# A fused attention and four-expert kernel: g_norm loaded as one row, batch 0's key-value products in two banks, and chunk 7 of the first expert with a two-level down product

## The chip, the cores and the metric

The kernel runs on one core of a Trainium2 chip. A core has a matmul engine (TensorE, PE in the profile; PEld is its weight load), three engines for elementwise work (VectorE or DVE, ScalarE or ACT, GpSimd or POOL), and SyncE (SP), which here only issues DMA transfers; GpSimd issues some too. Data lies in HBM, in the on-chip SBUF (128 partitions), and in the accumulators of TensorE, the PSUM, which has eight banks. The metric is the device time of one execution in microseconds (us); the time before is 1660.72 us, the median of three runs (1660.16 to 1660.84).

## The reference

First a linear attention for 8 batches of 8 heads, 576 rows and 64 columns, then a sum of four experts over the 4608 rows of 512 columns that it makes:

```python
kv = np.einsum('bhsd,bhse->bhde', k, v)
out = np.einsum('bhsd,bhde->bhse', q, kv)
rms = np.sqrt(np.mean(out * out, axis=-1, keepdims=True) + 1e-06)
attn = out / rms * g_norm
x = attn.transpose(0, 2, 1, 3).reshape(B * S, H * D)

p = domain_probs / (domain_probs.sum(-1, keepdims=True) + 1e-09)
for e in range(4):
    h = np.maximum(x @ w1[e], 0.0)
    out += p[:, e:e + 1] * (h @ w2[e])
```

Everything is float32; w1[e] is 512 x 1024, w2[e] 1024 x 512. The two expert products hold nearly all the multiplications.

## The kernel before

**Tiling.** The rows are cut into nine chunks of 512: chunks 0 to 7 are the first 512 rows of each batch, chunk 8 collects the 64 rows that each batch has left. For each expert and each chunk there is an *up* product (x by w1, then relu) and a *down* product (h by w2, times the probability, added to the output). The four experts follow each other, so there are 36 steps s = 9 e + chunk; the down product of a step is keyed 1.2 steps later than its number, beside the up product of the next one.

**Products.** Both products use Winograd's form of Strassen's scheme: seven products of half-size blocks in place of eight. Up products do so at two levels from step 1 on (`up`: seven outer products of seven inner ones, each with 128 columns). Down products do so at one level in `down` (seven products of 256 columns, for each of two row halves) and at two levels in `down_deep` (49 products of 128 columns in groups of two outer products). Steps 1 to 7 are *mixed*: `down(..., mixed=True)` does five outer products at one level and hands the other two, (4, 2), to `down_deep`. From step 8 to step 34 all goes through `down_deep`. The price of a level is sums and differences of blocks before and after: those of x and h are made on VectorE and GpSimd (helper `combine`, line 501), those of w1 and w2 once per expert. `w2y` is the kind of buffer that holds the inner sums of a w2 block, seven of them per expert; `inner[e](products, key)` plans them.

**Opening.** The attention of batch 0 (`opening`) is written apart, since nothing is there to hide it. For each of four head pairs it loads q, k and v (SP, line 507, 288 KB each), turns q (line 801), sums the key-value products of both heads into one PSUM bank (line 816), turns the last 64 rows of q (line 820), copies the four 64x64 quadrants that q's product needs out of that bank, two by ScalarE (line 833) and two by VectorE (line 831), multiplies q by them (line 855), scales the rows by their inverse root mean square (`scaled`: squares on ScalarE, line 732; row sums on VectorE, line 739; root, lines 699 to 711; scaling, line 751), and turns the result (line 870) into x, where ScalarE multiplies by g_norm on the way out of PSUM (line 876). The first expert's up product of chunk 0 (`up_plain`, plain products of 512 columns) starts when the first pair is there. Until the first loads are in, TensorE is kept running by small products of an identity (line 1793). The attentions of batches 1 to 7 (`attention`) are made one chunk ahead, among the products: key-value product (line 1031), q's product (lines 1058 and 1067), row sums (line 971), scaling (line 980), turning (lines 1099 and 1120).

**g_norm and the probabilities.** g_norm's 64 values are wanted one per partition, in both halves, in `gcol`: `load_gains` (line 1733) issues two GpSimd transfers of 64 partitions by one element. `norm_probs` loads the probabilities into `p_all` by ten GpSimd transfers (lines 522 to 531), and VectorE divides each by its row's sum (lines 535 to 538).

**Order.** All work is entered as operations of a `Plan` with a key (the step, with a fraction), a cost for each engine that can do it, and the buffers read and written. `Plan.layout` derives a due time for each, and places them by a model of the engines, the DMA and the shared SBUF port (`port=True` keeps VectorE and GpSimd operations that share it apart; a GpSimd operation of this kind also waits for the last such VectorE instruction). For each step it tries `TRIES` = 8 random variations of the due times and keeps the one that leaves TensorE least idle. Buffers are assigned as the order is made: kinds such as `big`, `xf`, `small`, `w2y` and the PSUM kinds `u1`, `u2`, `db`, `ab` (two banks each) have a fixed number of slots; `later` lists memory that becomes slots of another kind once its first users are done. The program's order on every engine, and which of two engines does a sum, thus follow from the whole plan.

Of the kernel before, what the change touches and what calls it, by code (L numbers as in the profile page):

```python
# [41 lines left out]
class Plan:  # L42
# [51 lines left out]
    def layout(self, slots, later, idle, idle_banks, idle_until):  # L94
# [265 lines left out]
def kernel(  # L360
# [76 lines left out]
    for kind, n in BANKS.items():  # L437
# [22 lines left out]
        (("small", "q"), "w2y", [small_home[:, 2 * i * NT:2 * (i + 1) * NT] for i in range(2)]),  # L460
# [53 lines left out]
    def norm_probs(key):  # L514
# [257 lines left out]
    def opening(key, span, rem):  # L772
# [11 lines left out]
        for hp in range(NPAIR):  # L784
# [9 lines left out]
            bank, kbank = Buf("ab", f"qT{n}"), Buf("ab", f"kv{n}")  # L794
# [17 lines left out]
            def key_values(eng, bank=kbank, kt=kt, vt=vt, qt=qt):  # L812
                for j in range(J):
                    for r in range(2):
                        half, cols = slice(r * D, (r + 1) * D), slice(j * D, (j + 1) * D)
                        nc.tensor.matmul(  # L816
                            bank.ap[half, 0:D], lhsT=kt.ap[half, cols], rhs=vt.ap[half, cols],
                            start=(j == 0), stop=(j == J - 1), skip_group_check=True,
                        )
                nc.tensor.transpose(bank.ap[0:D, P:2 * P], qt.ap[:, (J - 1) * D:J * D], ident[:])  # L820

            plan.add(at(hp), {"PE": 1.3}, key_values, reads=[qt, kt, vt], writes=[kbank])
            left_q = Buf(None, f"ql{n}")

            def spread(eng, bank=kbank, to=kv, shift=0):
                for r in range(2):
                    c = r ^ shift
                    src = bank.ap[r * D:(r + 1) * D, 0:D]
                    dst = to.ap[c * D:(c + 1) * D, r * D:(r + 1) * D]
                    if shift:  # L830
                        done = nc.vector.tensor_copy(out=dst, in_=src)
                    else:
                        done = nc.scalar.activation(out=dst, in_=src, func=ACT.Copy)
                return done

            plan.add(at(hp), {"ACT": 0.42}, spread, reads=[kbank], parts=[kv])
            plan.add(
                at(hp), {"DVE": 0.35}, lambda eng, spread=spread: spread(eng, shift=1),
                reads=[kbank], parts=[kv],
            )  # L840
# [3 lines left out]
                    out=qT.ap[0:D, NT:NT + P], in_=bank.ap[0:D, P:2 * P], func=ACT.Copy),  # L844
                reads=[kbank], parts=[left_q], holds=[qT],
            )
            lefts.append(left_q)
            raw = Buf("raw", f"raw{n}")

            def attend(eng, raw=raw, kv=kv, qT=qT):  # L850
                for i in range(2):
                    for r in range(2):
                        for c in range(2):
                            half, at = slice(c * D, (c + 1) * D), r * HN + i * P
                            nc.tensor.matmul(  # L855
                                raw.ap[c][:, (2 * i + r) * D:(2 * i + r + 1) * D],
                                lhsT=qT.ap[half, at:at + P], rhs=kv.ap[half, r * D:(r + 1) * D],
                            )

            plan.add(at(hp + 0.4), {"PE": 0.7}, attend, reads=[qT, kv], writes=[raw])  # L860
# [887 lines left out]
    for e in range(E):  # L1748
        for i in range(NCH):
# [95 lines left out]
```

## Time and profile before

| | before |
|---|---|
| median of three runs | 1660.72 us |
| the profiled execution | 1657.95 us |
| its span, first to last instruction | 1656.2 us |
| PE busy | 1647.5 us (99% of the span) |
| DVE / ACT / POOL busy | 1232.4 / 980.0 / 701.4 us |
| read from HBM / written | 153.95 / 74.19 MB |

The profile is of one execution. A group's name says line, engine, operation, and output<-inputs by the program's names. A wait's row says who waited for whom, the total in us, how often, and the longest. Matmuls overlap, so one that is listed with 1.04 us for 16 passes takes less from its start to the start of the next; a float32 matmul is listed as two passes. Line numbers are those of the kernel before unless "after" is said; in the changed kernel the same lines lie up to 17 further down.

### The profile page before, as it was taken

The page shows a single profiled execution, that of the slowest core. Times are in us where ns is not written, and L with a number is a line of the kernel's source. Part 1 is how long each engine was busy: PE and PEld are TensorE (multiplying, and loading weights), DVE is VectorE, ACT ScalarE, POOL GpSimd, SP SyncE. Part 2 cuts the span into 40 slices and gives each one's busy share as a digit, 9 for nine tenths or more (in the row PEclk, how much of TensorE's full clock was granted, in tenths as well). Part 3 has the DMA queues.
Part 4 walks back from the last instruction along what each step waited for, and adds up shares of the span by engine and source line. Part 5 has one row for each costly group of instructions (what it writes and reads, how often), then busy time and mean ns, then how long its engine had stood idle before and what let it go on. Part 6 is the DMA issues. An engine that isn't in the chain of part 4 may idle for free.

```text
span 1656.2 us, 66292 instructions
## 1 busy us (share of the span) xinstructions
PE 1647.5 (99%) x28854; PEld 1557.0 (94%) x28854; DVE 1232.4 (74%) x2166; ACT 980.0 (59%) x2429; POOL 701.4 (42%) x665
## 2 busy tenths in 40 slices
PE   9999999999999999999999999999999999999998
PEld 5688888888899999999999999999999999999996
DVE  5777778776877778777778777777778787777774
ACT  3465555555456666666566666666666566666662
POOL 4443233223344454553345554343355545444341
PEclk9999999999999999999999999999999999999999
DMA  9875665524475354444558445444577544444442
GB/s 230 218 204 158 191 182 153 157 101 173 146 198 140 99 127 118 131 118 118 155 147 192 116 113 126 109 109 110 141 191 174 122 119 117 117 108 112 117 104 52
DMA packets 202763, 232.43 MB, mean 140 GB/s; under 512 B 92840, under 2 KB 142440, under 8 KB 202472
## 3 DMA queue, kind: packets, MB, share of 16 engines
q1 hardware_dynamic: 178856, 191.41, 38.4%
q0 software_dynamic: 23616, 36.78, 14.3%
q8 instruction: 226, 3.70, 0.9%
q14 instruction: 65, 0.53, 0.1%
HBM read 153.95 MB, written 74.19 MB: 138 GB/s over the span
## 4 chain that ended last, share of the span: by engine, by line
PE 97%; DMA 2%; SPq 1%; DVE 0%; issue 0%; ACT 0%; DVEq 0%
PE u L478 47%; PE db L478 32%; PE ab L478 15%; PE ab L1031 1%; PE ab L1099 1%; PE ab L1058 1%; DMA big<-in_moe_w_dram 1%; SPq L507 1%; DMA big<-in_q_dram 1%; DMA kv<-in_v_dram 0%; PE db L855 0%; PE db L1067 0%; PE ab L1120 0%; DMA kv<-in_k_dram 0%; PE ab L816 0%; PE ab L870 0%
## 5 line engine op out<-in xcount | busy, mean ns | idle before, releaser
L501 DVE TENSOR_TENSOR big<-big,big 128x1024 f32<-128x1024 f32 (+1 forms) x550 | 499.5, 927 | 27.2 <-ACT big L1296 12.0
L478 PE MATMUL u<-xf,big 128*64 128x128 f32 x7072 | 513.6, 273 | 0.0
L478 PEld LDWEIGHTS u<-xf,big 128*64 128x64 f32 x7072 | 412.9, 137 | 5.1 <-issue 0.7
L478 PE MATMUL u<-xf,w1y 128*64 128x128 f32 x5304 | 392.7, 273 | 0.0
L478 PE MATMUL db<-big,big 128*64 128x128 f32 (+1 forms) x4304 | 360.2, 308 | 0.5 <-ACT snap L1650 0.5
L1340 DVE TENSOR_TENSOR big<-u,snap 128x256 f32<-128x256 f32 x454 | 190.9, 422 | 206.3 <-PE u L478 150.7
L478 PEld LDWEIGHTS u<-xf,w1y 128*64 128x64 f32 x5304 | 310.6, 137 | 2.9 <-issue 0.8
L478 PEld LDWEIGHTS db<-big,big 128*64 128x64 f32 x4304 | 263.1, 137 | 40.8 <-issue 1.7
L1332 ACT ACTIVATE snap<-u 128x256 f32<-128x256 f32 x490 | 188.0, 384 | 183.2 <-PE u L478 160.3
L501 POOL TENSOR_TENSOR big<-big,big 128x256 f32<-128x256 f32 (+1 forms) x143 | 200.9, 1407 | 166.2 <-DVE big L501 81.2
L1332 ACT ACTIVATE big<-u 128x256 f32<-128x256 f32 x454 | 173.3, 383 | 66.0 <-PE u L478 41.9
L501 POOL TENSOR_TENSOR big<-big 128x512 f32<-128x512 f32 (+1 forms) x90 | 110.5, 1228 | 143.6 <-DVE big L501 88.7
L1650 ACT ACTIVATE snap<-db 128x256 f32<-128x256 f32 (+1 forms) x230 | 82.5, 359 | 136.9 <-PE db L478 123.3
L1296 ACT ACTIVATE big<-big 128x1024 f32<-128x1024 f32 x134 | 140.9, 1051 | 5.6 <-DVE big L501 4.9
L1503 POOL DMA_DIRECT2D out_dram<-big x118 | 102.1, 1102 | 43.3 <-ACT big L1480 35.9
L1658 DVE TENSOR_TENSOR big<-ab,snap 128x256 f32<-128x256 f32 x166 | 69.9, 421 | 66.5 <-ACT snap L1650 35.7
L1332 ACT ACTIVATE u<-u 128x256 f32<-128x256 f32 x245 | 90.9, 372 | 35.8 <-PE u L478 24.3
L1688 POOL TENSOR_TENSOR big<-big 128x512 f32<-128x512 f32 x25 | 31.9, 1276 | 146.1 <-DVE big L501 128.5
L478 PE MATMUL ab<-big,big 128*64 128x128 f32 (+1 forms) x1344 | 93.8, 278 | 0.0
L501 DVE TENSOR_TENSOR big<-big 128x512 f32<-128x512 f32 (+1 forms) x114 | 90.3, 797 | 2.3 <-POOL big L501 1.8
L478 PE MATMUL db<-w2y,big 128*64 128x128 f32 x1248 | 91.8, 273 | 0.0
L1480 ACT ACTIVATE big<-big,p_all 128x256 f32<-128x256 f32 x192 | 90.9, 500 | 1.4 <-POOL big L1688 0.7
(200 smaller groups left out, 2360.4 us busy)
## 6 DMA issues: line engine op xcount, KB each, us to landing
xf<-x SPq DMA_DIRECT2D x104, 512.0 KB, 3.6
xf<-x_h SPq DMA_DIRECT2D x85, 256.0 KB, 3.3
xf<-x SPq DMA_DIRECT2D x78, 256.0 KB, 3.6
out_dram<-big POOLq DMA_DIRECT2D x78, 256.0 KB, 6.2
x<-xf SPq DMA_DIRECT2D x36, 512.0 KB, 3.4
big<-in_moe_w_dram SPq DMA_DIRECT2D x30, 512.0 KB, 6.1
x_h<-big SPq DMA_DIRECT2D x18, 512.0 KB, 3.5
big<-in_moe_w_dram POOLq DMA_DIRECT2D x18, 512.0 KB, 7.3
```

What stands on the lines that cost most here:

```text
L478: nc.tensor.matmul(out_[cols], lhsT=lhsT[:, cols], rhs=rhs, **kw)
L501: lambda eng: adder(eng).tensor_tensor(out=out_(), in0=a(), in1=b(), op=op),
L507: key, SPC, lambda eng: nc.sync.dma_start(out=dst(), in_=src), reads=reads,
L1031: nc.tensor.matmul(bank.ap[r * D:(r + 1) * D, o * D:(o + 1) * D], lhsT=ks[r], rhs=vs[r], start=(j == 0), stop=(j == len(sets) - 1), skip_g ...
L1296: lambda eng: nc.scalar.activation(out=b.ap[:], in_=b.ap[:], func=ACT.Relu),
L1332: lambda eng: nc.scalar.activation(out=where(), in_=ps.ap[:, 0:HN], func=ACT.Copy),
L1340: lambda eng: nc.vector.tensor_tensor(out=block(whole, a, t), in0=src.ap[:, 0:HN], in1=add_.ap[:], op=ALU.add),
L1480: lambda eng: nc.scalar.activation(out=cell(i, half), in_=ap(), func=ACT.Copy, scale=prob()),
L1503: nc.gpsimd.dma_start(out=dst, in_=cell(i)[parts, :], accum_op=ALU.add)
L1650: lambda eng: nc.scalar.activation(out=where(), in_=group_of(ps.ap), func=ACT.Copy),
L1658: lambda eng: nc.vector.tensor_tensor(out=cell(tq, dq), in0=group_of(src.ap), in1=group_of(add_.ap), op=ALU.add,),
L1688: lambda eng: adder(eng).tensor_tensor(out=whole(to), in0=whole(a), in1=whole(b), op=ALU.add),
```

## The change

Five edits to batch 0's start and one further on:

- g_norm is loaded by SP as one row of 64 values into the first partition of `p_all`'s memory, behind the first q, k and v. Two one-column matmuls against an identity turn it into a PSUM bank, VectorE copies it to `gcol`. The loads of the probabilities then wait for this turn.
- The two heads' key-value products go to two banks, of kinds `u2` and `u1` (before: one of kind `ab`). ScalarE copies both quadrants from the first bank, VectorE both from the second.
- q's product is two operations: one needs only the two quadrants on the diagonal of the copied block, the other the two beside it. For the first two pairs each product is cut into 64 columns of weights.
- The division of the probabilities is keyed 0.9 steps later and counts as a user of the shared port.
- For the steps below 3, forty variations are tried in place of eight.
- Step 7 (the eighth chunk of the first expert) goes through `down_deep` as a whole; its remaining five `w2y` sums are keyed at 6.8 in place of 8.2, and two `w2y` slots become free when `q` is done, and no longer only when `small` is done too.

```diff
-            for n in range(self.TRIES):
+            for n in range(self.TRIES * (5 if step < 3 else 1)):
...
-        (("small", "q"), "w2y", [small_home[:, 2 * i * NT:2 * (i + 1) * NT] for i in range(2)]),
+        (("q",), "w2y", [small_home[:, 2 * i * NT:2 * (i + 1) * NT] for i in range(2)]),
...
-            nc.vector.tensor_tensor(
+            return nc.vector.tensor_tensor(
...
-        plan.add(key, {"DVE": 1.5}, norm, reads=[probs], writes=[probs])
+        plan.add(key + 0.9, {"DVE": 1.5}, norm, reads=[probs], writes=[probs], port=True)
...
-            bank, kbank = Buf("ab", f"qT{n}"), Buf("ab", f"kv{n}")
+            bank = Buf("ab", f"qT{n}")
+            kbank = [Buf(f"u{2 - r}", f"kv{n}_{r}") for r in range(2)]
...
-                            bank.ap[half, 0:D], lhsT=kt.ap[half, cols], rhs=vt.ap[half, cols],
+                            bank[r].ap[half, 0:D], lhsT=kt.ap[half, cols], rhs=vt.ap[half, cols],
...
-            plan.add(at(hp), {"ACT": 0.42}, spread, reads=[kbank], parts=[kv])
-            plan.add(
-                at(hp), {"DVE": 0.35}, lambda eng, spread=spread: spread(eng, shift=1),
-                reads=[kbank], parts=[kv],
-            )
+            kv_own, kv_other = Buf(None, f"kvo{n}"), Buf(None, f"kvx{n}")
+            for other in range(2):
+                to, at_ = (kv_own, kv_other)[other], slice(other * D, (other + 1) * D)
+                for r in range(2):
+                    c = r ^ other
+                    plan.add(
+                        at(hp), {"DVE": 0.235} if r else {"ACT": 0.24},
+                        lambda eng, r=r, c=c, at_=at_, kbank=kbank, kv=kv: nc.vector.tensor_copy(
+                            out=kv.ap[c * D:(c + 1) * D, at_],
+                            in_=kbank[r].ap[r * D:(r + 1) * D, 0:D]) if r
+                        else nc.scalar.activation(
+                            out=kv.ap[c * D:(c + 1) * D, at_],
+                            in_=kbank[r].ap[r * D:(r + 1) * D, 0:D], func=ACT.Copy),
+                        reads=[kbank[r]], parts=[kv, to],
+                    )
...
-            def attend(eng, raw=raw, kv=kv, qT=qT):
+            raw, wide = Buf("raw", f"raw{n}"), D if hp < 2 else P
+
+            def attend(eng, raw=raw, kv=kv, qT=qT, other=0, wide=wide):
                 for i in range(2):
...
+                    for c in range(2):
+                        r, half = c ^ other, slice(c * D, (c + 1) * D)
+                        at = r * HN + i * P
+                        for g in range(0, P, wide):
                             nc.tensor.matmul(
...
+                                raw.ap[c][g:g + wide, (2 * i + r) * D:(2 * i + r + 1) * D],
+                                lhsT=qT.ap[half, at + g:at + g + wide],
+                                rhs=kv.ap[half, other * D:(other + 1) * D],
...
-    def load_gains(eng):
+    gain_row, gain_bank = probs, Buf("u1", "gain_bank")
+    grow = p_all[0:1].rearrange("p n e -> p (n e)")[:, 0:D]
+    plan.add(
+        -2.95, SPC, lambda eng: nc.sync.dma_start(out=grow, in_=g_norm.unsqueeze(0)),
+        writes=[gain_row], kb=1)
+
+    def turn_gains(eng):
         for i in range(P // D):
-            nc.gpsimd.dma_start(out=gcol[i * D:(i + 1) * D, :], in_=g_norm.unsqueeze(1))
-
-    plan.add(-2.85, {"POOL": 2.5}, load_gains, writes=[gains], kb=1)
+            nc.tensor.matmul(
+                gain_bank.ap[i * D:(i + 1) * D, 0:1], lhsT=grow, rhs=ident[0:1, 0:1])
...
-            if s == NCH - 1:
-                inner[e]((1, 6, 7, 5, 3))
+            if s == NCH - 2:
+                inner[e]((1, 6, 7, 5, 3), 6.8)
...
-            if NCH - 1 <= s < E * NCH - 1:
+            if NCH - 2 <= s < E * NCH - 1:
                 down_deep(s, e, c)
             else:
-                down(s, e, c, 1 <= s < NCH)
+                down(s, e, c, 1 <= s < NCH - 2)
```

More of the change, by code (lines that the diff above doesn't have):

```diff
@@ L816, in key_values @@
                         nc.tensor.matmul(
[L817 removed]
+                            bank[r].ap[half, 0:D], lhsT=kt.ap[half, cols], rhs=vt.ap[half, cols],
                             start=(j == 0), stop=(j == J - 1), skip_group_check=True,
                         )
[L820 to L822 removed]
+                nc.tensor.transpose(bank[1].ap[0:D, P:2 * P], qt.ap[:, (J - 1) * D:J * D], ident[:])
@@ L823, in opening @@
+            plan.add(at(hp), {"PE": 1.3}, key_values, reads=[qt, kt, vt], writes=kbank)
             left_q = Buf(None, f"ql{n}")
-            def spread(eng, bank=kbank, to=kv, shift=0):
+            kv_own, kv_other = Buf(None, f"kvo{n}"), Buf(None, f"kvx{n}")
+            for other in range(2):
+                to, at_ = (kv_own, kv_other)[other], slice(other * D, (other + 1) * D)
                 for r in range(2):
[L827 to L834, printed above, removed]
@@ L843, in opening @@
                 lambda eng, bank=kbank, qT=qT: nc.scalar.activation(
[L844 to L845 removed]
+                    out=qT.ap[0:D, NT:NT + P], in_=bank[1].ap[0:D, P:2 * P], func=ACT.Copy),
+                reads=kbank[1:], parts=[left_q], holds=[qT],
             )
             lefts.append(left_q)
[L848 to L850 removed]
+            raw, wide = Buf("raw", f"raw{n}"), D if hp < 2 else P
+            def attend(eng, raw=raw, kv=kv, qT=qT, other=0, wide=wide):
                 for i in range(2):
[L852 to L854 removed]
+                    for c in range(2):
+                        r, half = c ^ other, slice(c * D, (c + 1) * D)
+                        at = r * HN + i * P
+                        for g in range(0, P, wide):
                             nc.tensor.matmul(
[L856 to L860 removed]
+                                raw.ap[c][g:g + wide, (2 * i + r) * D:(2 * i + r + 1) * D],
+                                lhsT=qT.ap[half, at + g:at + g + wide],
+                                rhs=kv.ap[half, other * D:(other + 1) * D],
+                            )
+            plan.add(
+                at(hp + 0.4), {"PE": 0.36 if wide == D else 0.5}, attend, reads=[qT, kv_own], holds=[kv], writes=[raw])
+            plan.add(
+                at(hp + 0.4), {"PE": 0.36 if wide == D else 0.5}, lambda eng, attend=attend: attend(eng, other=1),
+                reads=[qT, kv_other], holds=[kv], parts=[raw])
             x = Buf("big", f"xg{n}")
@@ L1729 @@
     gains = Buf(None, "gains", gcol)
-    def load_gains(eng):
-        for i in range(P // D):
-            nc.gpsimd.dma_start(out=gcol[i * D:(i + 1) * D, :], in_=g_norm.unsqueeze(1))
-    plan.add(-2.85, {"POOL": 2.5}, load_gains, writes=[gains], kb=1)
+    gain_row, gain_bank = probs, Buf("u1", "gain_bank")
+    grow = p_all[0:1].rearrange("p n e -> p (n e)")[:, 0:D]
+    plan.add(
+        -2.95, SPC, lambda eng: nc.sync.dma_start(out=grow, in_=g_norm.unsqueeze(0)),
+        writes=[gain_row], kb=1)
+    def turn_gains(eng):
+        for i in range(P // D):
+            nc.tensor.matmul(
+                gain_bank.ap[i * D:(i + 1) * D, 0:1], lhsT=grow, rhs=ident[0:1, 0:1])
+    plan.add(-1.99, {"PE": 0.3}, turn_gains, reads=[gain_row], writes=[gain_bank])
+    plan.add(
+        -1.85, {"DVE": 0.15},
+        lambda eng: nc.vector.tensor_copy(out=gcol[:], in_=gain_bank.ap[:, 0:1]),
+        reads=[gain_bank], writes=[gains])
     opening(-2.0, 1.3, 0.1)
```

## The prediction

> **What bounds the kernel now.** I read the page first: busy time and the chain that ended last.
>
> ```profile
> span 1656.2 us, 66292 instructions
> PE 1647.5 (99%) x28854; PEld 1557.0 (94%) x28854; DVE 1232.4 (74%) x2166; ACT 980.0 (59%) x2429; POOL 701.4 (42%) x665
> ...
> PE 97%; DMA 2%; SPq 1%; DVE 0%; issue 0%; ACT 0%; DVEq 0%
> ```
>
> TensorE (PE) is busy or named as the cause nearly everywhere, so two things count: matmul work removed, and time at the ends in which TensorE does nothing useful. The waits of PE name the idle part (total, times, longest):
>
> ```profile
> PE ab L1793 <- POOL ident masks.py:199: 1.4, 1, 1.4
> PE ab L801 <- DMA big<-in_q_dram: 1.0, 1, 1.0
> PE ab L1099 <- DVE ss L971: 0.8, 1, 0.8
> PE db L478 <- ACT snap L1650: 0.5, 1, 0.5
> PE ab L1031 <- DMA kv<-in_v_dram: 0.3, 1, 0.3
> PE db L855 <- ACT kv L833: 0.2, 1, 0.2
> ```
>
> After 80 us only one wait of 0.5 us is left. Anything to win outside the products lies in the first 80 us. The chain in that stretch (start, length):
>
> ```profile
> 4.04 8.96 DMA big<-in_q_dram
> ...
> 14.80 1.20 PE ab L816 x36
> ...
> 16.66 0.36 PE db L855 x2
> 17.02 0.00 issue
> 17.02 1.14 PE db L855 x14
> ...
> 20.18 1.87 PE u L478 x8
> ```
>
> So the opening is paced by loads until about 14.8 us and by TensorE afterwards; the first eight expert passes end at 22.05. The stage view (length, then busy time; last DMA share and GB/s) shows that the loads do not run evenly:
>
> ```profile
> 4.50:7.50 3.00, 3.00 (x59) 2.59 (x56) 0.00 (x0) 0.60 (x1) 0.00 (x0) 1.00 0.61 160
> 7.50:16.50 9.00, 7.73 (x151) 6.55 (x147) 3.61 (x11) 4.22 (x14) 2.18 (x3) 1.00 1.05 395
> ```
>
> In the slow 3 us the software queue, which only the two g_norm loads use by then, is moving its packets: 61 of them between 3.8 and 7.5 us. The two loads were issued at 1.5 to 2.7 us and landed 5.4 and 6.0 us after issue.
>
> **The skill.** "TensorEngine Tiling (Array Packing)", "Tiling Modes" and "Key Properties": 64x64 gives four tiles, 64x128 two, and different tiles may load weights and multiply in parallel. The trace agrees: L1058 (64x64, four tiles) does 64 passes in 0.99 us, 15.5 ns each; L855 (64 rows by 128 columns) 16 in 1.04 us, 65 ns. "PSUM — Partial Sum Buffer", "PSUM bank collisions": two engines may not touch one bank and quadrant together. The timeline shows ScalarE starting its copies out of the bank only when VectorE's end, though it needs nothing of VectorE's:
>
> ```profile
> 8.77 0.47 DVE L831 COPY kv<-ab 64x64 f32<-64x64 f32 x2 [7.90 <-PE ab L820]
> ...
> 9.34 0.46 ACT L833 ACTIVATE kv<-ab 64x64 f32<-64x64 f32 x2 [2.24 <-DVE kv L831]
> ```
>
> "DMA: Bandwidth & Descriptors", "Rules for kernel authors": a strided last dimension costs a descriptor per element; g_norm laid along partitions is that, 128 of 4 bytes. "SBUF — State Buffer", "Who interferes with whom": a VectorE tensor_scalar can be blocked for a whole GpSimd instruction. Here L536, 36 elements wide, took 2.10 us beside a GpSimd add of 2.37.
>
> **Part by part.**
>
> *Chunk 7's down products.* Before: five of seven at 256 columns, two at two levels. The unit rows, from around 380 us, where the gap from one start to the next is the cost:
>
> ```profile
> 379.35 1.04 PE L478 MATMUL db<-w2y,big 128*64 128x128 f32 x16
> 380.23 0.61 PE L478 MATMUL u<-small,w1y 128*64 128x128 f32 x8
> ...
> 386.34 1.90 PE L478 MATMUL db<-big,big 128*64 128x256 f32 x16
> 388.07 0.61 PE L478 MATMUL u<-small,big 128*64 128x128 f32 x8
> ```
>
> 16 passes of 256 columns take 388.07 - 386.34 = 1.73 us, 108.1 ns each; 8 of 128 take about 0.437 us, 54.6 ns each. TensorE's instruction order, built for both kernels, has 80 fewer 256-column and 140 more 128-column instructions, two passes each: -160 x 0.1081 + 280 x 0.0546 = -17.30 + 15.29 = **-2.0 us**. Other product counts are equal, as is the number of returns from attention work to products (53), so nothing offsets it. The price is elsewhere: VectorE +24 instructions, ScalarE +10, by count. Step 7 has no attention left to do, and between 325 and 450 us VectorE was busy 16.4 to 21.0 us of each 25, so I cost it at nothing; without that cover, see the slower rival. The w2 sums for five products are only moved, a step earlier (their buffers are freed when q is done, no longer when q and small are).
>
> *Opening, loads.* g_norm becomes one 256-byte row on SP, behind the first v. SP's later issues move 0.47 us back (the issue step, 2.14 - 1.67); the third v load now waits for the first v's landing (6.8 us) instead of the first k's, 1.1 us later than before. Both hide behind queued loads: that v was 8.8 us from issue to landing. What leaves is the small packets. If they are what halves the rate, 3.0 us at 160 GB/s moves 480 KB, which 395 GB/s moves in 1.2 us: all loads behind land up to 1.8 us sooner. If they are not: 0. A loss is excluded down to the 0.47 us issue slot.
>
> *Opening, TensorE.* The key-value product keeps its two 64x64 tiles, so I leave it at 1.20 us (upper gain, if one shared bank was the limit: down to 36 x 0.0155 = 0.56 us, 0.6 us per pair). The copies now run on two engines from two banks: done about 0.5 us sooner. q's product for pairs 0 and 1 becomes 32 passes on four tiles, 32 x 0.0155 = 0.5 us for 1.04; pairs 2 and 3 stay at 1.04 in two operations. The g_norm turn, two one-column matmuls, falls in TensorE's wait for the second q (8.7 us); its VectorE copy of 64x1 per half stands ahead of the first row sum, at most 0.2 us, and the result is needed only at 18.8. GpSimd loses two issues (1.26 us) in a stretch where it waits for w1 until 12.3 anyway; p_all's ten loads now wait for the turn, long past, and go out one 2.36 us sum earlier.
> With loads unchanged: second q's product 13.7 to 14.25; third key-value from 14.65 (its v lands at 14.5) to 16.1; fourth q turned 16.6; first x turned 17.2; half a product 17.7; fourth key-value 19.15; other half 19.65; eight passes, 21.5. That is -0.55 against 22.05. With loads 1.8 us sooner TensorE becomes the limit from the first key-value on (its fillers end at 7.2 whatever lands): the same sums end at 19.85, -2.2. I take loads 1.2 us sooner: third key-value at 13.45, end at 20.4: **-1.65**. The row sums that x needs keep up: first x ready near 14.4.
>
> *The wait at 58.8.* TensorE waits 0.76 us there because VectorE first did a w2 sum held up to 51.1 us by late loads, then the probability norm with its 2.1 us blocked instruction. In the changed order that w2 sum is GpSimd's, and the norm counts as a user of the shared port. With the durations of before, its row sums of chunk 1 end near 47.4, the root (ScalarE, behind two relus) 48.8, the four small steps 49.6, the norm 50.9 (0.3 + 0.2 + 0.4 + 0.3) and the scaling 52.1, where it was 58.06; TensorE arrives near 56.4: **-0.76**, even with TensorE early (0 if VectorE is late again). GpSimd's four w2 sums end at about 58.3 as its third did before it began; they are used from 62 us on.
>
> Sum: -2.0 - 1.65 - 0.76 = -4.4. Against the profiled execution (1657.95 us; span 1656.2 and 1.75 around it) that is 1653.5; the runs' median lies 2.8 above that execution, so 1660.72 - 4.4 = **1656.3**. The tail, 5 us after the last matmul, has the same order of instructions in both.
>
> **Rivals.** (B) *Only the products shrink.* The packets are not what slows the loads, and what TensorE gains early it loses waiting near 60 to 80 us, where DMA share is 0.82 to 0.97 and a key load already costs 0.32. For it: DMA is that full. Against: most waits of SP there are on TensorE itself (6.8 us on L1099) and move with it. Time: 1660.72 - 2.0 - up to 0.55, about 1658.4.
> (C) *Slower: VectorE late in step 9.* More tries were allowed for the first steps, so the order after them is new everywhere. Adding durations of VectorE's rows (1.23, 0.69, 0.42, 0.28 us by width) between its up-product sums: the second half of step 9 holds 21.7 us of work, before 12.6, in about 21.4 us of products. At the usual 76% busy that takes 28.6 us, 7.2 too long: 1656.3 + 7.2 = 1663.5. It decides from 4.4 us on. Against: neighbouring halves hold 18.5 and 16.0, room to work ahead, and 21.5 us halves occurred before with no wait.
> (D) *More:* key-value products gain from two banks too, or the waits at 78 and 1626 us go: 1653.5 to 1655.
> That the change does not do what it says is excluded for the products by the counts.
>
> **Numbers.** A 0.48 (1655.0 to 1657.6, at 1656.3), B 0.24, C 0.19, D 0.09. The bound of 0.2%, about what a measurement of this kernel can tell from no change, is 3.3 us: 1657.4 and 1664.0. Faster: A's 0.45 and D, 0.54. Same: A's 0.03, B, 0.07 of C, 0.34. Slower: 0.12. Range 1654.8 to 1662.0: A, B, half of D, a quarter of C.
>
> **What would show it.** Right: the stage from 4.5 to 7.5 us near 395 GB/s; eight expert passes done near 20.4 us; no wait of L1105 on VectorE near 57; no 256-column db products for chunk 7 and TensorE still busy throughout 375 to 450 us. Wrong: a wait of PE on VectorE or GpSimd after 80 us, or a DMA wait of over 1 us before it.

## The result, and the profile after

| | before | after |
|---|---|---|
| median | 1659.84 us (15 runs, 1658.35 to 1660.89) | 1655.60 us (15 runs, 1653.56 to 1660.74) |
| the profiled execution, its span | 1657.95, 1656.2 us | 1657.52, 1655.8 us |

The ratio of after to before is 0.9979, with a 95% interval of 0.9972 to 0.9986: 3.5 us less by the ratio (2.3 to 4.6), 4.2 by the medians. The two profiled executions differ by only 0.4 us, since the one of before lies 1.9 us below its median and the one of after 1.9 above. So the two traces show which waits went and came, but the size of the opening's gain has to come from many executions.

Page of after, span and busy time, then the chain's shares:

```profile
span 1655.8 us, 66574 instructions
PE 1644.6 (99%) x29010; PEld 1559.3 (94%) x29010; DVE 1240.3 (75%) x2190; ACT 983.1 (59%) x2439; POOL 712.5 (43%) x665
...
PE 96%; DMA 2%; SPq 1%; issue 0%; DVE 0%; ACT 0%
```

TensorE is still the bound: 2.9 us less busy. The waits of PE in after (total, times, longest):

```profile
PE ab L1037 <- DMA big<-in_v_dram: 1.7, 1, 1.7
PE ab L1810 <- POOL ident masks.py:199: 1.4, 1, 1.4
PE ab L802 <- DMA big<-in_q_dram: 1.3, 1, 1.3
PE ab L1037 <- DMA kv<-in_v_dram: 1.0, 2, 0.8
PE u L478 <- ACT big L732: 0.6, 1, 0.6
PE db L478 <- ACT snap L1656: 0.5, 1, 0.5
PE u L817 <- DMA big<-in_v_dram: 0.3, 1, 0.3
```

The wait on VectorE (0.8 us, L1099 of before, L1105 now) is gone. In its place L1037, the key-value product of batches 1 and 2, waits for v. The stages of the opening (length, PE, PEld, DVE, ACT, POOL busy, clock, DMA share, GB/s):

```profile
4.50:7.50 3.00, 3.00 (x74) 2.71 (x72) 0.00 (x0) 0.60 (x1) 0.00 (x0) 1.00 1.04 346
7.50:16.50 9.00, 7.41 (x185) 6.26 (x181) 4.72 (x15) 5.21 (x17) 2.18 (x3) 1.00 1.02 378
```

The slow 3 us have gone from 160 to 346 GB/s. By queue, from 4.5 to 7.5 us (packets, MB, share of the 16 DMA engines), before and then after:

```profile
q1 hardware_dynamic: 232, 0.48, 59.5%
q0 software_dynamic: 54, 0.00, 1.1%
...
q1 hardware_dynamic: 516, 1.04, 103.7%
```

The prediction counts 128 descriptors of four bytes for the two g_norm loads. The trace shows packets, and the pages have 64 fewer on the software queue without these loads (23616 before, 23552 after and in experiment 3). In the slow stage they took 1.1% of the engines' time, and the large loads 59.5% in place of 103.7%. So the small packets did not crowd the large ones out by their own time: the engines stood partly idle. What holds the large loads up is not shown.

TensorE's timeline, six rows of the opening and of batch 1 (start, duration, in brackets the idle time before it):

```profile
8.95 0.69 PE L856 MATMUL db<-kv,big 64*64 64x64 f32 x32
9.47 1.23 PE L817 MATMUL u<-big,big 64*64 64x64 f32 x36
12.19 0.66 PE L802 MATMUL ab<-ident,big 128*128 128x128 f32 x4 [1.26 <-DMA big<-in_q_dram]
13.80 1.26 PE L817 MATMUL u<-big,big 64*64 64x64 f32 x36 [0.33 <-DMA big<-in_v_dram]
...
19.40 1.94 PE L478 MATMUL u<-big,big 128*64 128x512 f32 x8 [0.63 <-ACT big L732]
...
44.67 0.80 PE L1037 MATMUL ab<-big,big 120*64 120x64 f32 x20 [1.66 <-DMA big<-in_v_dram]
```

q's product of pair 0 takes 9.47 - 8.95 = 0.52 us for its 32 passes. The first eight expert passes end at 21.34 (before 22.05). The chain that ended last shows how the 1.66 us come about (start, length):

```profile
20.55 1.77 SPq L507
24.45 4.19 DMA big<-in_v_dram
29.28 1.45 SPq L507
31.85 5.51 DMA small<-in_q_dram
37.42 7.12 DMA big<-in_v_dram
```

SP's queue, with the sixteen small loads of q for the next batch in it, comes to the second v of batch 1 only at 37.42, just after a small load of q that was issued at 31.85 has landed, and that v lands 7.1 us later.

**Where the time went, by equal work.** The next table compares the start of the n-th pass of an up product with its start in the trace of before, in us; negative is earlier than before. Rows are chosen where both kernels have done equal product work, but for the last two, where those with the new chunk 7 have done 2.0 us less.

| up-product pass, and its time in before | after | after, again | row alone | all but chunk 7 | chunk 7 alone |
|---|---|---|---|---|---|
| first, 20.1 us | -0.70 | -2.17 | -0.97 | -0.93 | +4.13 |
| 101st, 50.4 us | +1.13 | +2.31 | -0.26 | -0.98 | +4.13 |
| 151st, 67.6 us | +0.18 | +1.36 | -0.13 | -1.92 | +3.14 |
| 793rd, 152.0 us | +1.07 | +2.16 | -0.07 | -1.07 | +3.47 |
| 3537th, 497.3 us | -0.91 | +0.17 | -0.07 | -1.08 | +1.48 |
| last, 1649.6 us | -0.34 | +0.74 | -0.07 | -1.08 | +1.98 |

All that differs between the two executions of the changed kernel comes before 80 us. From 152 to 497 us each kernel with the new chunk 7 gains 1.98 to 1.99 us (but for the one of experiment 8, whose own order loses 0.8 us in between), and no other gains anything. Afterwards those kernels give 0.25 to 0.6 us back, in steps of 0.1 to 0.25 us.

### The profile page after: what moved, and what is told of

The parts are those of the page before. It is cut to its first block, busy times and chain, and to the rows that moved or that the text cites. A ratio compares the mean times of both kernels' runs of the same rounds, so it can differ in the third digit from the quotient of the medians.

```text
span 1655.8 us, 66574 instructions
## 1 busy us (share of the span) xinstructions
PE 1644.6 (99%) x29010; PEld 1559.3 (94%) x29010; DVE 1240.3 (75%) x2190; ACT 983.1 (59%) x2439; POOL 712.5 (43%) x665
## 3 DMA queue, kind: packets, MB, share of 16 engines
q0 software_dynamic: 23552, 36.78, 14.7%
## 4 chain that ended last, share of the span: by engine, by line
PE 96%; DMA 2%; SPq 1%; issue 0%; DVE 0%; ACT 0%
PE u L478 47%; PE db L478 32%; PE ab L478 15%; SPq L507 1%; DMA big<-in_v_dram 1%; PE ab L1064 1%; PE ab L1105 1%; PE ab L1037 1%; DMA big<-in_q_dram 0%; DMA small<-in_q_dram 0%; DMA kv<-in_v_dram 0%; PE db L1073 0%; PE ab L1126 0%; DVE big L1493 0%; PE ab L910 0%
## 5 line engine op out<-in xcount | busy, mean ns | idle before, releaser
L478 PE MATMUL db<-big,big 128*64 128x128 f32 (+1 forms) x4152 | 342.5, 304 | 0.5 <-ACT snap L1656 0.5
L501 POOL TENSOR_TENSOR big<-big,big 128x256 f32<-128x256 f32 (+1 forms) x164 | 231.2, 1413 | 178.9 <-DVE big L501 76.3
L478 PEld LDWEIGHTS db<-big,big 128*64 128x64 f32 x4152 | 252.9, 137 | 36.6 <-issue 1.2
L501 POOL TENSOR_TENSOR big<-big 128x512 f32<-128x512 f32 (+1 forms) x99 | 124.1, 1254 | 190.6 <-DVE big L501 117.6
L1656 ACT ACTIVATE snap<-db 128x256 f32<-128x256 f32 x236 | 84.4, 358 | 137.4 <-PE db L478 124.9
L1509 POOL DMA_DIRECT2D out_dram<-big x112 | 97.5, 1121 | 43.1 <-ACT big L1486 35.1
L478 PE MATMUL db<-small,big 128*64 128x128 f32 (+1 forms) x1344 | 102.1, 274 | 0.0
L478 PE MATMUL ab<-big,big 128*64 128x128 f32 (+1 forms) x1392 | 97.8, 276 | 0.0
L478 PE MATMUL ab<-kv,big 128*64 128x128 f32 x1280 | 88.4, 273 | 0.0
```

What stands on the lines that cost most here:

```text
L478: nc.tensor.matmul(out_[cols], lhsT=lhsT[:, cols], rhs=rhs, **kw)
L501: lambda eng: adder(eng).tensor_tensor(out=out_(), in0=a(), in1=b(), op=op),
L1509: nc.gpsimd.dma_start(out=dst, in_=cell(i)[parts, :], accum_op=ALU.add)
L1656: lambda eng: nc.scalar.activation(out=where(), in_=group_of(ps.ap), func=ACT.Copy),
```

## The experiments

Each ratio is to the kernel before on the same chip, with its 95% interval; 0.001 is 1.66 us.

**1. All but chunk 7** (changed kernel, with the old chunk 7):

```diff
-            if s == NCH - 2:
-                inner[e]((1, 6, 7, 5, 3), 6.8)
+            if s == NCH - 1:
+                inner[e]((1, 6, 7, 5, 3))
...
-            if NCH - 2 <= s < E * NCH - 1:
+            if NCH - 1 <= s < E * NCH - 1:
...
-                down(s, e, c, 1 <= s < NCH - 2)
+                down(s, e, c, 1 <= s < NCH)
...
-        (("q",), "w2y", [small_home[:, 2 * i * NT:2 * (i + 1) * NT] for i in range(2)]),
+        (("small", "q"), "w2y", [small_home[:, 2 * i * NT:2 * (i + 1) * NT] for i in range(2)]),
```

> The changed kernel with chunk 7 mixed again as before (and the five w2 sums and the two w2y slots where they were); TensorE's order is the changed kernel's up to the sixth step. Theory (products are what counts): 2.0 us slower than the changed kernel, so a ratio to the kernel before near 0.999. Rival (the new orders at the start are what counts, the products hide behind something else): no slower than the changed kernel, ratio 0.998. From step 7 on the lag to the kernel before, at equal up products, stays what it was at step 6.

Measured: 1656.91 us, 0.9987 (0.9981 to 0.9994), 1.3 us above the changed kernel's ratio. From step 7 on its lag to the kernel before stays what it was (-1.07 and -1.08 in the table), as expected.

**2. Chunk 7 alone** (kernel before, with the same four edits the other way round):

> The kernel before with chunk 7 at two levels and nothing else of the change; TensorE's order is that of before up to the fifth step. Theory: 2.0 us faster than before (160 passes of 256 columns less, 280 of 128 more), ratio 0.9988, no new wait of TensorE in the steps 7 to 9. Rival (VectorE late in step 9): less than 1 us gained or a loss, with a wait of TensorE on VectorE or GpSimd between 400 and 520 us.

Measured: 1658.42 us, 0.9991 (0.9983 to 0.9999): 1.5 us faster (0.2 to 2.8). Its profiled execution began with 2.8 us of waits for q, and then the granted clock was 0.50 from 15 to nearly 22 us, whence the +4.13 above, but from 152 to 497 us it gains exactly 1.99. No wait of PE on VectorE or GpSimd appears after 80 us: the slower rival of the prediction, VectorE late in step 9, does not occur. The steps that give 0.5 us back come in this kernel (from +1.48 to +1.98 in the table) and in every other with the new chunk 7; all of these show 0.25 us or so of it between 642 and 648 us, and none of the kernels with the old chunk 7 does. So chunk 7 nets about -1.5, as timed. What the steps are stays open: the profile names no wait of PE between 600 and 1500 us.

**3. No g_norm loads** (kernel before; what it leaves out, its expectation says):

```diff
         for i in range(P // D):
-            nc.gpsimd.dma_start(out=gcol[i * D:(i + 1) * D, :], in_=g_norm.unsqueeze(1))
+        nc.gpsimd.memset(gcol[:], 1.0)
```

> The kernel before with the two g_norm loads left out: GpSimd sets the column to one instead, so the multiplication by g_norm is left out of the result. Instruction order and buffers are those of before. Theory (the small packets slow the loads): the stage from 4.5 to 7.5 us moves at least 330 GB/s where it moved 160, the third pair's q product begins about 1 us sooner, and the time is 0.5 to 1.5 us shorter. Rival (the slow stage is something else, such as the start of the loads): stage and time as before.

Measured: 1658.06 us, 0.9989 (0.9981 to 0.9997), 1.75 us by the medians, and 1.8 (0.5 to 3.2) by the ratio. The stage, in this kernel:

```profile
4.50:7.50 3.00, 3.00 (x73) 2.72 (x71) 0.00 (x0) 0.60 (x1) 0.00 (x0) 1.00 0.96 346
```

**4. The two strided loads back** (changed kernel, into a column that nobody reads):

```diff
+    gspare = const.tile([P, 1], F32, name="gspare")
...
         make_identity(nc, ident[:])
+        for i in range(P // D):
+            nc.gpsimd.dma_start(out=gspare[i * D:(i + 1) * D, :], in_=g_norm.unsqueeze(1))
```

> The changed kernel with the two strided g_norm loads issued by GpSimd as well, into a column that nothing reads. Theory (small packets): the stage from 4.5 to 7.5 us falls back to 160 to 200 GB/s, first expert passes about 1 us later than in the changed kernel, total 0.5 to 1.2 us more than it. Rival: stage and total as in the changed kernel. If the wait for the second pair's v of batch 1 (1.66 us at 42.9 in the changed kernel's profile) is what limits the start, the total stays equal though the stage slows down.

Measured: 1656.91 us, 0.9981 (0.9974 to 0.9988): by the ratio only 0.3 us above the changed kernel, by the medians 1.3. The same stage:

```profile
4.50:7.50 3.00, 2.61 (x57) 2.27 (x55) 0.00 (x0) 0.60 (x1) 0.00 (x0) 1.00 0.57 168
```

Experiments 3 and 4 switch the slow stage off and on by these two loads and nothing else: 346 GB/s without, 168 with them. In time, the loads' cost in the changed kernel is not shown: 0.3 us by the ratio is less than the 0.5 to 1.2 expected, but the intervals allow more. This profile has the wait for v of batch 1 too (1.6 us), and the expectation says that the total could then stay equal. The first expert pass starts 0.60 us earlier than before even with the slow loads. This compares one execution with one other, and two of the changed kernel differ by 1.47 us there, so it doesn't fix the worth of the opening's other edits.

**5. The row alone** (kernel before, with the g_norm row, its turn and its copy in place of `load_gains`, as in the diff of the change; nothing else):

> The kernel before with one part of the change: g_norm as one row, with its turn and copy; key-value products, q's product, norm, tries and chunk 7 as before. TensorE's and VectorE's order up to 60 us is that of before but for the turn, and the probabilities' loads stay behind two sums. The kernel before without any g_norm load was 1.75 us faster. Theory 'the packets are the opening's gain': the stage from 4.5 to 7.5 us moves 310 GB/s or more in place of 160, and the time is 1.2 to 1.9 us below before. Rival 'the turn and the row give it back': the stage is as fast, the time within 0.6 us of before.

Measured: 1658.17 us, 0.9988 (0.9981 to 0.9994): 2.0 us faster (1.0 to 3.2), which agrees with no loads at all. No loss by the turn and the row is seen. This gain rests on the timed runs: in the traces the row's first expert pass is 0.97 us early, and from the 793rd pass on only 0.07 us of that are left; a wait of 0.36 us for batch 1's second v is one part of the loss. In the row the number of pieces and the issuing queue (SP's for GpSimd's) change together. Which of the two matters was not tested. Its stage:

```profile
4.50:7.50 3.00, 3.00 (x68) 2.72 (x66) 0.00 (x0) 0.60 (x1) 0.00 (x0) 1.00 1.05 313
```

**6. One bank and one q product again** (changed kernel, with `key_values`, the copies and `attend` of before):

```diff
-            bank = Buf("ab", f"qT{n}")
-            kbank = [Buf(f"u{2 - r}", f"kv{n}_{r}") for r in range(2)]
+            bank, kbank = Buf("ab", f"qT{n}"), Buf("ab", f"kv{n}")
...
-            raw, wide = Buf("raw", f"raw{n}"), D if hp < 2 else P
+            raw = Buf("raw", f"raw{n}")
```

> The changed kernel with one part undone: the two heads' key-value products of batch 0 go to one bank of kind ab again, two copies by ScalarE and two by VectorE as before, and q's product is one operation of 128 columns of weights; the g_norm row, the order rules and chunk 7 stay. Theory 'TensorE's part of the opening counts' (the prediction's 0.55 us at equal loads): for pairs 0 and 1 two times 0.52 us come back, and the copies end 0.5 us later; eight expert passes end 0.5 to 1.1 us later than in the changed kernel's profile (21.27 us there), and the time is 0.5 to 1.1 us above the changed kernel's. Rival 'loads set the opening': TensorE waits for the second q at 12.2 us and for v at 13.5 us whatever comes before, so eight passes end within 0.3 us of 21.3 and the time is within 0.3 us.

Measured: 1656.52 us, 0.9982 (0.9975 to 0.9988), not to be told from the changed kernel. The first expert pass starts 1.03 us earlier than before, inside the spread of the kernels with the new products (0.04 to 2.17). The eight passes end at 21.02 us, as the "loads set the opening" rival expects, but not by the waits that it names: with the old products and fast loads (here and in experiments 3 and 5) TensorE waits for no load between 7 us and the first expert pass, which starts at 19.0 to 19.1. With the new products it waits for q and v and starts at 17.9 to 20.1, 19.0 in the middle. So the shorter products mostly wait for the next load, and no gain of theirs in time is shown.

**7. The division of the probabilities as before** (changed kernel):

```diff
-        plan.add(key + 0.9, {"DVE": 1.5}, norm, reads=[probs], writes=[probs], port=True)
+        plan.add(key, {"DVE": 1.5}, norm, reads=[probs], writes=[probs])
```

> The changed kernel with the division of the probabilities as before: 0.9 steps earlier, and no user of the shared port. The order is planned anew from about 40 us on. Theory 'the norm's place made TensorE wait for VectorE': its small step (36 elements) takes about 2 us again in place of 0.18, TensorE waits for VectorE by about 0.8 us at its transposes near 57 us, the time is 0.8 us above the changed kernel's. Rival 'which engine had the w2 sum made it': the small step is slow again, but VectorE's scaling is done before TensorE arrives near 57 us; no wait of TensorE on VectorE, time within 0.3 us of the changed kernel's.

Measured: 1657.35 us, 0.9983 (0.9975 to 0.9991). GpSimd's sum, VectorE's small step and TensorE's transposes in its timeline:

```profile
52.77 2.36 POOL L501 TENSOR_TENSOR big<-big,big 128x1024 f32<-128x1024 f32 x1 [2.11 <-DVE rt L711]
...
53.08 2.08 DVE L536 TENSOR_SCALAR tot<-tot 128x36 f32<-128x36 f32 x1
...
58.28 1.25 PE L1105 MATMUL ab<-ident,small 128*128 128x128 f32 x8 [1.54 <-DVE ss L977]
```

The small step starts under GpSimd's sum and ends when that ends (55.13 and 55.16). TensorE waits 1.54 us. In the changed kernel the same step is free:

```profile
53.17 0.18 DVE L536 TENSOR_SCALAR tot<-tot 128x36 f32<-128x36 f32 x1
```

The Trainium skill has the mechanism, in "SBUF — State Buffer", "Who interferes with whom": where both need the shared ports, whichever of the two engines issues second is blocked for the whole instruction of the first. The trace agrees to 0.03 us. So the norm's edit does what the prediction says of it. It is not all that makes TensorE wait there: experiment 6 has the edit, and still waits 0.48 us for VectorE. In time the two kernels are not told apart (0.7 us by the ratio). This kernel's new order has no wait for v near 44 us, which may offset the one on VectorE.

**8. Eight tries** (changed kernel, `TRIES * (5 if step < 3 else 1)` back to `TRIES`):

> The changed kernel with eight variations in place of forty for the first steps. Its order is that of the changed kernel up to about 60 us and another one after it. Expected: up to 60 us the same course, so that its waits on loads show how far two executions of one order differ (the changed kernel's second batch waited 1.66 and 0.8 us for v, 1.26 us for the second q, 0.63 us at the first expert product); no wait of TensorE on VectorE near 57 us. If the forty tries are worth something, new waits of 0.5 us or more come between 60 and 100 us; if not, none do, and the time is within 0.4 us of the changed kernel's.

Measured: 1656.96 us, 0.9985 (0.9978 to 0.9991). No wait on VectorE near 57 us, and no new wait above 0.7 us between 60 and 100. The wait for v came again, with 1.46 us. It lies 1.0 us above the changed kernel by the ratio, inside the intervals; 0.8 us of the chunk's gain are missing in its order between 152 and 497 us. That the forty tries are worth anything is not shown.

**9. The changed kernel once more:**

> The changed kernel once more, nothing altered, as the measure for the other three. Its first profile and two kernels with the same early order waited 1.5 to 1.7 us for v at the second key-value product of batch 1 (near 44 us), one with that order did not wait. If the wait belongs to the order it comes again with 1.4 to 1.7 us; if it is how far executions differ, anything from 0 to 1.7. Time: 1655 to 1657 us.

Measured: 1656.15 us, 0.9978 (0.9968 to 0.9988). In its profile the opening does nearly all that the prediction's upper bound allows, and then the wait takes it back:

```profile
17.94 1.94 PE L478 MATMUL u<-big,big 128*64 128x512 f32 x8
...
43.95 0.69 PE L1037 MATMUL ab<-big,big 120*64 120x64 f32 x16 [2.18 <-DMA big<-in_v_dram]
```

Eight passes end at 19.9 us, 2.17 sooner than before (the prediction's bound was 19.85); by the 101st pass it is 2.3 us behind before. It has lost 4.5 us in between, twice the wait. The stages behind the wait show the other half (clock, DMA share and GB/s are the last three):

```profile
44.00:46.00 2.00, 1.82 (x24) 0.81 (x24) 0.14 (x1) 0.28 (x1) 2.00 (x2) 0.94 1.10 345
46.00:48.00 2.00, 2.00 (x70) 1.93 (x70) 0.00 (x0) 0.00 (x0) 1.33 (x2) 0.50 1.10 347
48.00:50.00 2.00, 2.00 (x18) 0.85 (x14) 1.14 (x3) 1.64 (x4) 0.57 (x1) 0.71 1.07 264
```

TensorE's clock was halved from some 45.8 to 49.2 us (worked out from the three means): the 64 passes of L1064 take 1.99 us there, and 1.16 in the first profile of the changed kernel, where the wait was 1.66 and the clock stayed at 1.00. The Trainium skill describes this in "TensorE: Matmul & The Clock Gate", "Part 1: The HAM clock gate": a monitor halves the clock after an idle window of about 3.4 us, and gives it back after a busy one. Here less sufficed: waits of 2.18 and 2.50 us were each followed by a halved clock (experiments 9 and 10), and so were one of 2.11 and one of 1.83 that had shorter waits some 3 to 4 us before them (experiments 2 and 11). Waits up to 1.78 us standing alone were not.

**10. The probabilities' loads behind two more sums of GpSimd** (changed kernel; the order is changed after planning):

```diff
+    n = next(i for i, op in enumerate(order) if getattr(op.fn, "__name__", "") == "load_all")
+    sums = [i for i in range(n + 1, len(order)) if order[i].eng == "POOL"]
+    order.insert(sums[2 - 1], order.pop(n))
```

> The changed kernel with one move: the ten loads of the probabilities are issued behind the next two sums of GpSimd, as late as before the change or one sum later (near 33 us in place of 28.3); all other orders are the same. Theory 'their small packets slow the loads of batch 1': the second key-value product's wait for v near 44.7 us (1.66 us in the changed kernel's profile) falls below 0.5 us, batch 1's later waits do not grow by as much, and the time is 1 to 1.5 us below the changed kernel's. Rival 'those waits are how far executions differ': the wait is anywhere from 0 to 1.7 us, and the time is within 0.4 us of the changed kernel's.

Measured: 1660.62 us, 1.0003 (0.9995 to 1.0011), some 4 us slower than the changed kernel. The second of those sums waits for its operands until 42.6 us, so the loads were issued at 44.9 and not near 33, and landed at 57.0. No wait for the second v of batch 1 is left, but VectorE stands in front of the division:

```profile
57.03 0.30 DVE L535 TENSOR_REDUCE tot<-p_all 128x36 f32<-128x144 f32 x1 [6.06 <-DMA p_all<-in_moe_domain_probs_dram]
```

VectorE waits 6.06 us, and behind it the scaling, so TensorE's transposes wait 2.5 us. The granted clock is then 0.53 from 60 to 62 us and 0.61 from 62 to 64, which costs up to 1.7 us more.

**11. The loads behind one sum, and the division behind the three row sums that follow** (changed kernel, two moves of the same kind):

> The changed kernel with two moves: the ten loads of the probabilities behind GpSimd's next sum (issued near 42 us, landed near 54), and VectorE's division of them behind the row sums that follow, near 58 us in place of 53. The kernel with later loads alone waited 2.5 us for VectorE near 57 us, since the division stood in VectorE's queue until the loads landed at 57.0. Theory 'that place in the queue is the cost': without it no wait on VectorE near 57 us is left, and no wait for v near 44; time 1 to 1.6 us below the changed kernel's. Rival 'GpSimd, whose sums come 7 us later, is the cost': TensorE waits for GpSimd or VectorE between 60 and 100 us, time at or above the changed kernel's.

Measured: 1657.69 us, 0.9987 (0.9980 to 0.9994). No wait for v near 44 us, but 1.8 us at the next transposes (L1126 <- VectorE) and 0.9 at L1105, and again a halved clock behind them (0.50 from 66 to 68 us): the division's place was not the whole cost. GpSimd, kept for some 7 us by the probabilities' issues, and VectorE behind it come late for batch 1 in either place. Neither theory is met in full; the rival is nearer.

**12. The loads ahead of GpSimd's sum at 26 us** (changed kernel):

```diff
+    n = next(i for i, op in enumerate(order) if getattr(op.fn, "__name__", "") == "load_all")
+    sums = [i for i in range(n) if order[i].eng == "POOL"]
+    order.insert(sums[-1], order.pop(n))
```

> The changed kernel with one move: the ten loads of the probabilities are issued ahead of GpSimd's sum at 26.0 us instead of behind it, near 20 us, when the DMA share is 0.44 to 0.84; that sum starts 1.5 us later, and nothing else is altered. Theory 'their small packets slow q and v of batch 1': at 28 to 34 us the DMA share falls from 1.1 to 1.7 towards 1.0, v lands sooner, the wait near 44 us is below 0.5 us, and no wait on VectorE comes for it, unlike where the loads were put later; time 1 to 1.6 us below the changed kernel's in the same job. Rival 'executions differ': time within 0.4 us of it.

Measured: 1655.34 us, 0.9971 (0.9959 to 0.9982); the changed kernel once more (experiment 9) has 1656.15 and 0.9978, so the two are not told apart. The loads are issued at 19.5 to 26.5 us here. The wait for v is there with 1.8 us, and the DMA share at 28 to 34 us is 1.27 still: the wait does not need these loads to be issued at 28 to 35 us. That they play no part is not shown: it stays away in both kernels that issue them after 40 us (experiments 10 and 11), though also in experiments 1 and 6, with the loads at 28 us.

**What the wait for v hangs on.** Over the profiles, it goes with the time at which SP gets to that v. Start of its issue, and the wait before the second product:

| kernel | issued at, us | wait, us |
|---|---|---|
| one bank again; norm back; probabilities 42 us and later (two kernels); no g_norm loads | 34.9; 34.8; 33.9 and 35.3; 34.8 | 0 |
| row alone | 35.1 | 0.4 |
| all but chunk 7; before | 35.6; 35.9 | 0 |
| eight tries; strided loads back | 36.1; 36.7 | 1.5; 1.6 |
| changed kernel again; probabilities first; changed kernel | 36.9; 37.1; 37.4 | 2.2; 1.8; 1.7 |

The order on SP is the same in "one bank again" and in the changed kernel up to there. (Chunk 7 alone is left out: its whole start is 4 us late.) The sixteen small loads of q ahead of it, in two sets of eight, take 15.9 to 17.6 us together in the executions with a wait of over 1 us, and 13.5 to 15.5 in the others, but for 16.0 without g_norm loads, where they start earliest. This goes together, and was not varied by itself: why they are slower in most executions of the changed order is not settled. "All but chunk 7" has the changed kernel's order there and did not wait.

## Why the prediction was right, and which term was not

The time came out at 1655.6 us for 1656.3, on the forecast's side. Its steps one by one:

*Chunk 7's down products, -2.0.* Right in work: 1.98 to 1.99 us in every trace with this edit but that of experiment 8. As time it is about -1.5, for the 0.5 us of small steps later, which the prediction put at nothing ("so nothing offsets it"). Rival C's wait on VectorE did not come, and VectorE's cover held: PE was busy in all of 325 to 450 us.

*Opening, loads.* Right that the two loads halve the rate, shown by removing, adding and replacing them alone (346, 168 and 313 GB/s, for 160). That they do so by their packets is not shown: these are 64, with 1.1% of the engines' time in the slow stage, and the replacement changes the queue as well. The estimate of 395 GB/s was high: 279 to 349 in the eleven profiles without the loads.

*Opening, TensorE, -1.65.* The size was off. "TensorE becomes the limit from the first key-value on" failed for the shortened products: with fast loads it still waits for the second q (1.26 us in after, 0.3 to 1.4 in the other executions with that order) and for the third v (0.3 to 0.5). With the old products (experiments 3, 5 and 6) it held. After's profile has -0.70 at the eighth pass; by the start of the first expert pass, eight executions with the changed order of the opening and the row (the first profile, experiments 1 and 7 to 12) lie between -0.04 and -2.17, with -1.1 in the middle. The value at slow loads, -0.55, is near the one execution that tests it (-0.60 with the strided loads back), which can't confirm it to better than the 1.5 us by which executions differ there. A small slip: the prediction's own durations, from 13.45 on, end at 20.3 and not 20.4. The copies overlap as expected (for pair 0 in after, 8.03 to 8.49 us on ScalarE and 8.27 to 8.75 on VectorE). The q product's 0.5 us for 32 passes (0.52) and the unchanged key-value product (1.23 as listed) were right as prices, but no gain in time from them is shown.

*The wait at 58.8, -0.76.* It is gone, and the mechanism named is seen in experiment 7. The prediction then let the gain stand. It did not ask what comes next on the queues: batch 1's second v, whose landing near 43.3 to 45.4 us is set, by the chain of after, by SP and the loads and not by TensorE. This is the signal that the prediction named as wrong, a DMA wait of over 1 us before 80 us (as is the 1.26 us for the second q), and it came in five of six profiles with the changed order up to there and the probabilities' loads not later (the first profile and experiments 1, 4, 8, 9 and 12), with 1.5 to 2.2 us, and once with the halved clock on top. The second half of rival B, that what is gained early is lost waiting on loads, holds in part, at 44 us rather than 60 to 80.

*Tail.* Same in both: TensorE's last products run back to back, as before. Rival D (more) did not come: the key-value product is no shorter, and the wait near 78 us is still there.

In sum, by timed runs: the row alone -2.0, chunk 7 alone -1.5, everything but chunk 7 -2.2, all -3.5 by the ratio. The row and chunk 7 are nearly the whole change; two banks, the split q product, the norm and the tries net about -0.2, give or take some 1.5 us (an estimate from the two intervals, 1.0 to 3.2 us each). Undone one by one they cost 0.5, 0.7 and 1.0 us by the ratio (experiments 6 to 8), none clear of the noise. The forecast of -4.4 was 0.9 us too much by the ratio, and the start was 0.9 us too high (1660.72 from three runs, 1659.84 from fifteen): by the ratio, the two errors cancel. That the time was met so closely is luck.

No kernel tried here is shown to beat the changed one.

## What to carry to other kernels

A transfer of a few bytes to each of many partitions, issued by GpSimd, was dear here beside large loads that the first products wait for; loading such a vector as one row by SP and turning it on TensorE avoided this. When an opening gets shorter, follow each queue to the next load that is not moved by it, since TensorE only arrives there sooner, and a wait there can cost twice its length (4.5 us lost for one of 2.18). And where one profiled execution lies two microseconds off its median, a part of that size is measured by timing it alone, not by comparing two traces.

## What was not expected of the hardware

- Two g_norm loads of 64 four-byte values each cut the rate of the large loads beside them from 279 to 349 GB/s to 160 to 168 for 3 us, that is some 0.5 MB not moved for 512 bytes, while their own packets took 1.1% of the engines' time.
- A wait of TensorE of 2.1 to 2.5 us was followed by half the clock for about 3.4 us of the records, some 1.7 us of work lost, twice that in experiment 2; one of 1.8 us alone was not. Two executions with nearly the same opening and 1.78 and 2.18 us of wait (experiments 12 and 9) were 2.4 us apart by the 101st pass. Whether this is what spreads the unprofiled runs (1653.56 to 1660.74 for one kernel) no run here shows.
- Executions of one order differ by 1 to 2 us and more in the first 80 us (at the 793rd pass 1.1 us between the two of the changed kernel, 2.1 between the first of them and experiment 1); from 152 to 497 us, equal work took equal time within 0.02 us.
- The nine issues of the probabilities' loads (the description of the kernel and the prediction say ten) keep GpSimd 7 us (28.3 to 35.3), during which no sum runs there. Moved to 44.9 us, they made TensorE wait 2.5 us for VectorE, while no effect of their packets is shown.
